# Loading and multiplying the first four x tiles by pairs of feature chunks

## Chip, cores and metric

The kernel runs on one core of one Trainium2 chip. The metric is device time in microseconds, the median of several runs. The engines are TensorE (PE, with its weight loads shown apart as PEld), VectorE (DVE), ScalarE (ACT), GpSimd (POOL) and SyncE (SP), which here only issues DMAs; ACT issues some too.

## What is computed

Two independent parts share one input length of 2048 rows and a width of 1024, and their outputs are joined along the last axis. Part A is a diagonal state-space layer: a complex recurrence over time between two matrix products. Part B is attention over segments of 32 rows with 8 memory rows, whose first step is three projections of the rows:

```python
h = jnp.concatenate([mem, xs], axis=1)
q = jnp.einsum('btd,dhe->bhte', h, Wq)
k = jnp.einsum('btd,dhe->bhte', h, Wk)
v = jnp.einsum('btd,dhe->bhte', h, Wv)
```

The change lies in the start of `v` alone: x is 2048 x 1024, `Wv` is 1024 x 4096 (32 heads of 128).

## The kernel before

**What the start does.** The features (1024) are cut into KC = 8 chunks of 128, the rows into 16 tiles of 128, and the 4096 columns of `Wv` into 8 head blocks (`hb`) of 512. A tile of values is eight matmuls into one PSUM bank, one for each chunk: the stationary operand is a chunk of the turned rows (`b_xe`, features on partitions), the moving one the same chunk of `Wv`'s head block (512 columns). `v_mm` (L414) issues them. Two names of PSUM buffers alternate, psS and psP, with two banks each. Turned rows of tiles 4 to 15 come by DMA transposes (`load_x`, L369); the first four tiles are loaded as they stand (`load_rows`, L372), turned on PE by a product with the identity (`turn_rows`, L379, into psO) and copied to `b_xe` by DVE (L77).

**Loads.** SP and ACT each issue half of the first loads in turn (`q2`): for each tile its rows in two halves of the features, then two chunks of head block 0 of `Wv` (L406). After all four tiles follow head block 1 of `Wv` in two halves of 512 KB, and on SP three loads of 2 KB for `params` (L144), one of 16 KB with the memory rows `mem0` (L906), and five DMA transposes of x. Rows, weights and small loads share one SBUF tile name, `a_hs`. Eight completion semaphores are used in turn, so the third DMA of a queue that reuses one waits for the landing of the earlier DMA.

**Order of the work.** `kernel_main` issues warm-up matmuls on constants (L913), and then draws steps from the generator `values()`: `v_first` (the first four tiles of head block 0), `v_pair` for head block 1 on the same tiles, then both head blocks on the other tiles, then head blocks 2 to 7 between the steps of part A. After the seventh step it calls `params` (its first instruction is the matmul at L150, which turns the three parameter vectors) and `init` (L344, eight small matmuls that turn `mem0`). Matmuls of `v_mm` and transposes of `turn_rows` are held in program order by `keep_in_program_order`; the matmuls of `params` and `init` are not, and a scheduler at build time places them.

In `v_first` each tile is turned when its rows are there, and then those tiles that have been turned are multiplied with the chunks of weights that have been loaded:

```python
for t, todo in enumerate((((0, 0, 2),), ((0, 2, 4), (1, 0, 4)), ((0, 4, 6), (1, 4, 6), (2, 0, 6)),
                          ((0, 6, 8), (1, 6, 8), (2, 6, 8), (3, 0, 8)))):
    self.turn_rows(t, xr)
    for tt, c0, c1 in todo:
        self.v_mm(p[tt], tt, w, range(c0, c1))
```

ACT then copies the four banks to SBUF (L75) and SP stores them to DRAM.

Of the kernel before, what the change touches and what calls it, by code (L numbers as in the profile page):

```python
# [9 lines left out]
BF16 = mybir.dt.bfloat16  # L10
# [306 lines left out]
class PartB:  # L317
# [50 lines left out]
            if lo < hi:  # L368
                k.SP.dma_start(self.xe[:, :, lo:hi], self.x[0][lo + r:hi + r, :], transpose=True)  # L369

    def load_rows(self, t, xr, e, cs=slice(0, D)):
        self.k.tc.keep_in_program_order(e.dma_start(xr[:, t, cs], self.x[0][t * 128 + 64:t * 128 + 192, cs]))  # L372

    def turn_rows(self, t, xr):

        k = self.k
        pt = k.ps("O", (128, 2, 1024), BF16)
        for c in range(KC):
            k.tc.keep_in_program_order(k.PE.transpose(pt[:, c // 4, (c % 4) * 128:(c % 4) * 128 + 128], xr[:, t, c * 128:(c + 1) * 128], k.ident[:]))  # L379
        for i in range(2):  # L380
            k.copy("v", self.xe[:, 4 * i:4 * i + 4, t * 128:(t + 1) * 128], pt[:, i, 0:512].rearrange("p (c n) -> p c n", c=4))

    def sum_x(self, q, pool):

# [59 lines left out]
    def v_first(self, w, xr, e):  # L444

        k = self.k
        p = [k.ps("A") for t in range(4)]
        for t, todo in enumerate((((0, 0, 2),), ((0, 2, 4), (1, 0, 4)), ((0, 4, 6), (1, 4, 6), (2, 0, 6)),
                                  ((0, 6, 8), (1, 6, 8), (2, 6, 8), (3, 0, 8)))):
            self.turn_rows(t, xr)  # L450
            for tt, c0, c1 in todo:
                self.v_mm(p[tt], tt, w, range(c0, c1))
        for q in range(2):
            st = self.v_tile()
            for i in range(2):
                k.copy("s", st[:, i, :], p[2 * q + i][:])
                if i == 0:
                    yield
            self.v_st(0, q, st, e)
            yield  # L460
# [396 lines left out]
def check_consts(k):  # L857

    V, G = k.V, k.G
    k.fmask = k.cst.tile([L, 2, L], FP32, name="f_mask")  # L860
    G.memset(k.fmask[:], 1.0)
    G.affine_select(out=k.fmask[:, 0, :], in_=k.fmask[:, 0, :], compare_op=ALU.is_ge, fill=0.0, base=0,
                    pattern=[[-1, L]], channel_multiplier=1)
    G.memset(k.fmask[0:M, 0, :], 1.0)
    k.tc.keep_in_program_order(V.tensor_scalar(k.fmask[:, 1, :], k.fmask[:, 0, :], 1.0, 1.0e9, ALU.subtract, ALU.mult))


def kernel_main(tc, A_x, A_Lre, A_Lim, A_Bre, A_Bim, A_Cre, A_Cim, A_logdt, A_Dskip, B_x, B_mem0, B_Wq, B_Wk, B_Wv, B_Wo, out,
                force=False, dbg=None):
    with ExitStack() as ctx:  # L870
        k = K(tc, ctx)
# [4 lines left out]
        b = PartB(k, B_x, B_mem0, B_Wq, B_Wk, B_Wv, B_Wo, out)  # L876

        def pool(name, side, bufs=2):
            return tc.tile_pool(name=name, bufs=bufs, side=side, reuse_waits="tile")
# [7 lines left out]
        with pool("p1", "right") as p1:  # L887
            tmp = a.hsp.tile([128, 2 * PC * TB], BF16, name="a_hs", bufs=4)
            w01 = a.hsp.tile([128, 2 * PC * TB], BF16, name="a_hs", bufs=4)
            wvs = {i: w01[:, 4096 * i:4096 * i + 4096].rearrange("p (a b) -> p a b", a=KC) for i in range(2)}  # L890
            st0 = a.hsp.tile([128, 2 * PC * TB], BF16, name="a_hs", bufs=4)
            b.st0 = [st0[:, 1024 * i:1024 * i + 1024].rearrange("p (a b) -> p a b", a=2) for i in range(8)]
            a.pin = b.pin = True
            a.tab = a.wp = a.btp = b.vst = p1
            a.jf = b.rall[:, 0:TB + 1]
            xr = tmp[:, 4096:8192].rearrange("p (t d) -> p t d", t=4)
            q2 = (k.SP, nc.scalar)
            for t in range(4):
                for j in range(2):
                    b.load_rows(t, xr, q2[j], slice(j * 512, j * 512 + 512))  # L900
                for j in range(2):
                    b.load_wv(0, wvs[0], KC, q2[j], [2 * t + j])
            for j in range(2):
                b.load_wv(1, wvs[1], 2, q2[j], [j])
            a.load_params(tmp)
            k.SP.dma_start(tmp[0:M, 0:D], b.mem0[0])  # L906
            b.load_x(512, 1024)
            b.load_x(1024, 1536)
            b.load_x(1536, T)
            one = nc.const_aps.tensor(1.0, [128, 512], BF16)  # L910
            pw = k.ps("O")
            for i in range(7):
                k.PE.matmul(pw[:, i % 2, :], one[:, 0:128], one, start=True, stop=True)  # L913

            def values():
                yield from b.v_first(wvs[0], xr, k.SP)
                for hb, q in [(1, 0), (1, 1)] + [(hb, q) for q in range(2, 8) for hb in range(2)]:
                    yield from b.v_pair(hb, q, wvs[hb], k.SP)
                for hb in range(2, HB):
                    for q in range(8):  # L920
                        if q == 1 and hb + 1 < HB and hb + 1 not in wvs:
                            wvs[hb + 1] = b.load_wv(hb + 1)
                        yield from b.v_pair(hb, q, wvs[hb], k.SP)
            v = values()
            done = 0
            while done < 20:
                next(v); done += 1
                if done == 7:
                    a.params(p1, tmp)
                    b.init(tmp, k.ps('O')[:, 0, :])  # L930
                    a.bt = a.load_b(0)
                    a.load_x(0)
                    tabs = a.tables(0)
                if done == 18:
                    a.load_x(1)
                if done in (9, 14, 17):
                    next(tabs)
                if done in (11, 13, 15, 17, 19):
                    b.sum_x((done - 11) // 2, p1)
            a.tabs = a.ntabs  # L940
            oged = 0
            for n in range(PC * NB):
                pc, tb = n // NB, n % NB
                a.stage1(pc, tb)
                if n in (0, 1):
                    a.load_x(2 + n)
                    wvs[2 + n] = b.load_wv(2 + n)
                if tb == 1 and pc + 1 < PC:
                    nbt = a.load_b(pc + 1)
                want = 20 + 4 * (n + 1) if n < 4 else 36 + (92 * (n - 3) + 27) // 28  # L950
                half = done + 2
                while done < want:
                    next(v, None); done += 1
                    if done == half:
                        a.post(a.prev)
                while done >= 32 and oged < done // 16:
                    b.og(oged, wvs.pop(oged))
                    oged += 1
                if pc + 1 < PC:
                    if tb == 0:  # L960
                        tabs = a.tables(pc + 1)
                    else:
                        next(tabs)
                    if tb == 3:
                        a.tabs, a.bt = a.ntabs, nbt
                if n == 3:
                    a.pin = b.pin = False
                if n == 8:
                    masks(k)
                    check_consts(k)  # L970
                    dB = k.cst.tile([128, D], BF16, name="a_dB")
                    tc.keep_in_program_order(nc.scalar.dma_start(dB[:], A_Dskip.unsqueeze(0).to_broadcast([128, D])))
                if n == 28:
                    a.load_c(0, 0)
                if n == 29:
                    a.load_c(0, 1)
            a.post(a.last)
            k.V.memset(b.rall[:], 0.0)
            a.load_c(1, 0)
            a.load_c(1, 1)  # L980
# [20 lines left out]
        with pool("p3", "right") as p3:  # L1001
# [11 lines left out]
            for n, (hp, u) in enumerate(at):  # L1013
# [4 lines left out]
                if u == 4 and 8 <= hp < 12:  # L1018
                    w = k.w8((8, 512), "wo0")
# [57 lines left out]
@with_exitstack  # L1077
def kernel(
    ctx: ExitStack,
    tc: tile.TileContext,  # L1080
    A_x: bass.AP,
    A_Lambda_re: bass.AP,
    A_Lambda_im: bass.AP,
    A_B_re: bass.AP,
    A_B_im: bass.AP,
    A_C_re: bass.AP,
    A_C_im: bass.AP,
    A_log_dt: bass.AP,
    A_Dskip: bass.AP,
    B_x: bass.AP,  # L1090
    B_mem0: bass.AP,
    B_Wq: bass.AP,
    B_Wk: bass.AP,
    B_Wv: bass.AP,
    B_Wo: bass.AP,
    B_seg_len: bass.AP,
    out: bass.AP,
):
    assert int(B_seg_len) == SEG
    kernel_main(tc, A_x, A_Lambda_re, A_Lambda_im, A_B_re, A_B_im, A_C_re, A_C_im, A_log_dt, A_Dskip,  # L1100
                B_x, B_mem0, B_Wq, B_Wk, B_Wv, B_Wo, out)
# [35 lines left out]
```

## Time and profile before

| what | value |
|---|---|
| median of 5 runs | 1242.49 us (1241.62 to 1242.99) |
| profiled execution, its own time | 1242.26 us |
| its span, first to last instruction | 1240.5 us |
| busy: PE | 1231.4 us (99%) |
| busy: DVE, ACT, POOL | 611.0, 325.9, 199.9 us |
| DMA traffic | 153.95 MB, mean 124 GB/s |
| L414 matmuls, 128x512 | 379 ns in the record, 8 in 1.73 us |
| L379 transposes, 128x128 | 32, the first at 3.8 us, the last at 11.5 us |

Busy time counts an engine's own instructions; a matmul's record is longer than its distance to the next, since they are pipelined. Times in the timelines and in the chain are microseconds from the span's start. A bracket such as [0.50 <-DMA x] says how long the engine had been idle before the instruction, and what ended it.

### The profile page before, as it was taken

How to read it: one execution, taken by the hardware profiler on the slowest of the kernel's cores; microseconds unless marked ns; L12 is line 12 of the kernel's file. 1: busy time of each engine (PE TensorE's matmuls, PEld its weight loads, DVE VectorE, ACT ScalarE, POOL GpSimd, SP SyncE). 2: the span in 40 equal slices, each digit the busy share in tenths (PEclk: the TensorE clock that was granted, in tenths of full speed). 3: DMA queues.
4: the chain of work that ended last, by engine and by line, in shares of the span. 5: the costliest groups of instructions: out<-in, count | busy, mean ns of one | idle time of the engine just before them, and what ended most of it. 6: DMA issues, size and time to landing. Idle time of an engine off the chain costs nothing.

```text
span 1240.5 us, 19641 instructions
## 1 busy us (share of the span) xinstructions
PE 1231.4 (99%) x8078; PEld 655.2 (53%) x8148; DVE 611.0 (49%) x1124; ACT 325.9 (26%) x754; POOL 199.9 (16%) x284
## 2 busy tenths in 40 slices
PE   9999999999999999999999999999999999999998
PEld 4444444444455445566666665655565554454444
DVE  4889999999941122444444444444444550011000
ACT  3344434444310001333333323333333230000000
POOL 2000000000032140222222222222222330000000
PEclk9999999999999999999999999999999999999999
DMA  9942232332656558577768554645575469607000
GB/s 224 262 127 68 85 94 68 102 94 78 152 187 204 157 161 167 103 151 151 141 119 176 120 137 95 129 77 101 106 139 106 72 203 224 147 18 153 17 18 28
DMA packets 306056, 153.95 MB, mean 124 GB/s; under 512 B 147242, under 2 KB 299810, under 8 KB 305962
## 3 DMA queue, kind: packets, MB, share of 16 engines
q1 hardware_dynamic: 304138, 150.82, 52.5%
q10 hardware_dynamic: 1824, 1.84, 0.5%
q8 instruction: 65, 1.06, 0.4%
q14 instruction: 29, 0.24, 0.1%
HBM read 73.70 MB, written 44.71 MB: 95 GB/s over the span
## 4 chain that ended last, share of the span: by engine, by line
PE 99%; DMA 0%; issue 0%; SPq 0%; DVE 0%
PE psP L585 33%; PE psS L685 9%; PE psS L414 9%; PE psP L414 9%; PE psO L256 9%; PE psP L685 5%; PE psP L310 4%; PE psS L310 4%; PE psP L568 4%; PE psO L629 3%; PE psS L611 3%; PE psO L685 2%; PE psS L718 1%; PE psP L505 1%; PE psP L737 1%; PE psO L482 1%
## 5 line engine op out<-in xcount | busy, mean ns | idle before, releaser
L585 PE MATMUL psP<-b_xe,w 128*128 128x480 bf16 x2048 | 439.6, 366 | 0.0
L585 PEld LDWEIGHTS <-w 128*128 128x128 bf16 x2048 | 193.7, 98 | 183.5
L618 POOL TENSOR_TENSOR b_m<-b_e,maskB 99x396 bf16<-99x396 bf16 x160 | 139.4, 871 | 348.2 <-ACT b_e L614 348.2
L77 DVE CAST b_q<-psP 128x480 bf16<-128x480 f32 (+1 forms) x192 | 98.1, 532 | 145.5 <-PE psP L585 134.0
L414 PEld LDWEIGHTS <-b_xe 128*128 128x128 bf16 x1024 | 99.8, 98 | 121.0 <-DVE b_xe L77 1.1
L75 ACT ACTIVATE b_k<-psP 128x480 bf16<-128x480 f32 x128 | 73.1, 571 | 319.1 <-PE psP L585 319.1
L685 PEld LDWEIGHTS <-b_ol 128*128 128x128 bf16 x960 | 93.1, 98 | 109.4
L614 ACT ACTIVATE b_e<-psS 99x396 bf16<-99x396 f32 x176 | 87.4, 497 | 170.9 <-PE psS L611 165.6
L636 DVE TENSOR_TENSOR b_ot<-psO,b_rall 99x512 bf16<-99x512 f32 x176 | 121.7, 691 | 6.4
L256 PE MATMUL psO<-w,a_bt 128*128 128x512 bf16 x496 | 114.7, 379 | 0.8
L634 DVE RECIPROCAL b_rall<-psO 99x4 f32<-99x4 f32 x176 | 31.2, 177 | 132.9 <-PE psO L629 132.9
L685 PE MATMUL psS<-w,b_ol 128*128 128x512 bf16 x406 | 91.5, 379 | 0.6
L414 PE MATMUL psS<-w,b_xe 128*128 128x512 bf16 x378 | 90.1, 379 | 0.4
L414 PE MATMUL psP<-w,b_xe 128*128 128x512 bf16 x376 | 89.8, 379 | 0.4
L256 PEld LDWEIGHTS <-a_bt 128*128 128x128 bf16 x512 | 49.7, 98 | 59.0
L310 PEld LDWEIGHTS <-a_hs 128*128 128x128 bf16 x512 | 49.5, 98 | 58.3
L77 DVE CAST b_ost<-psS 128x512 bf16<-128x512 f32 x13 | 9.0, 692 | 125.4 <-PE psS L685 125.4
L629 PE MATMUL psO<-b_v,b_m 99*128 99x129 bf16 x704 | 70.4, 221 | 0.0
L611 PEld LDWEIGHTS <-b_k 128*128 128x128 bf16 x704 | 50.0, 98 | 33.9 <-DVE b_k L77 0.2
L611 PE MATMUL psS<-b_q,b_k 128*128 128x99 bf16 x704 | 60.1, 208 | 0.1
L75 ACT ACTIVATE b_vst<-psS 128x512 bf16<-128x512 f32 x56 | 33.4, 597 | 99.4 <-PE psS L414 70.2
L310 PE MATMUL psS<-w,a_hs 128*128 128x512 bf16 x245 | 57.3, 379 | 0.6
(203 smaller groups left out, 1095.6 us busy)
## 6 DMA issues: line engine op xcount, KB each, us to landing
b_v<-b_vx SPq DMA_DIRECT2D x16, 1056.0 KB
b_os<-b_ot SPq DMA_DIRECT2D x16, 960.0 KB
w<-in_B_Wv_dram SPq DMA_DIRECT2D x14, 1024.0 KB
b_vx<-b_vst SPq DMA_DIRECT2D x48, 256.0 KB
w<-in_B_Wo_dram SPq DMA_DIRECT2D x12, 1024.0 KB
w<-in_B_Wq_dram SPq DMA_DIRECT2D x16, 512.0 KB
w<-in_B_Wk_dram SPq DMA_DIRECT2D x16, 512.0 KB
a_xn<-in_A_x_dram SPq DMA_DIRECT2D x32, 128.0 KB
```

Of the source, the lines that this page charges most:

```text
L75: self.S.activation(out, in_, ACT.Copy)
L77: self.V.tensor_copy(out, in_)
L256: m = PE.matmul(u[:, i, :], self.bt[:, i, c, :], self.xT[tb][:, c, :], start=(c == 0), stop=(c == KC - 1))
L310: PE.matmul(py[:], self.hs[tb][:, pc, i, tt * 128:(tt + 1) * 128], self.ct[half, i][:, pc, :], start=(pc == 0 and i == 0), stop=(pc == PC ...
L414: m = self.k.PE.matmul(p[:], self.xe[:, c, t * 128:(t + 1) * 128], w[:, c, :], start=(c == 0), stop=(c == KC - 1))
L585: PE.matmul(p[:, 0:480], w[:, i * KC + c, hh * 128:(hh + 1) * 128], self.xe[:, c, 480 * q:480 * q + 480], start=(c == 0), stop=(c == KC - 1))
L611: PE.matmul(s[:, j * GW:(j + 1) * GW], kt[:, hh, g0:g0 + 128], qt[:, hh, g0:g0 + GW], start=True, stop=True)
L614: k.S.activation(e[:], s[0:GW, 0:4 * GW], ACT.Exp, scale=float(E) ** -0.5, accum_out=self.accE[0:GW, i:i + 1])
L618: k.G.tensor_tensor(v4(m[:, 0:4 * GW]), v4(e[:]), mask[0:GW, :, :].unsqueeze(2).to_broadcast([GW, 2, 2, GW]), ALU.mult)
L629: PE.matmul(o[:, gg, cs], m[:, j * GW:j * GW + 128], vt[:, 2 * u + gg, cs], start=True, stop=True)
L636: V.tensor_tensor(ot[:, 2 * u:2 * u + 2, :].rearrange("p g (h e) -> p g h e", h=2), oa[:, :, 1:257].rearrange("p g (h e) -> p g h e", h=2) ...
L685: k.PE.matmul(self.acc[t, half], ol[:, h8, tt * 128:(tt + 1) * 128], self.wo_half(half, h), start=(h == 0), stop=(h == H - 1))
```

## The change

The first four tiles are handled as two pairs of tiles (j = 0, 1) and four pairs of chunks (q = 0 to 3). A row load now brings two tiles with 256 features each, instead of one tile with 512; the bytes of one load stay 128 KB, the contiguous piece falls from 1024 to 512 bytes. The two queues alternate rows and weights: SP has the rows of the first tile pair and the odd chunks of `Wv`, ACT the even chunks and the rows of the second pair. `turn_rows` turns two chunks of two tiles (four transposes) and makes one DVE copy of 512 columns. `v_first` walks over q, with all four tiles at each. There is one warm-up matmul less.

```diff
+    def load_rows(self, j, q, xr, e):
+        cs = slice(256 * q, 256 * q + 256)
+        self.k.tc.keep_in_program_order(e.dma_start(
+            xr[:, 2 * j:2 * j + 2, cs], self.x[0][256 * j + 64:256 * j + 320, cs].rearrange("(i p) d -> p i d", p=128)))
+    def turn_rows(self, j, q, xr):
+        k = self.k
+        pt = k.ps("O", (128, 2, 256), BF16)
+        for c in range(2):
+            for i in range(2):
+                k.tc.keep_in_program_order(k.PE.transpose(
+                    pt[:, c, i * 128:i * 128 + 128], xr[:, 2 * j + i, 256 * q + 128 * c:256 * q + 128 * c + 128], k.ident[:]))
+        k.copy("v", self.xe[:, 2 * q:2 * q + 2, 256 * j:256 * j + 256], pt[:])
...
+        self.turn_rows(0, 0, xr)
+        for q in range(4):
+            if q > 0:
+                self.turn_rows(1, q, xr)
+            for t in range(2):
+                self.v_mm(p[t], t, w, (2 * q,))
+            if q == 0:
+                self.turn_rows(1, q, xr)
+            for t in range(2):
+                self.v_mm(p[t], t, w, (2 * q + 1,))
+            if q < 3:
+                self.turn_rows(0, q + 1, xr)
+            for t in range(2, 4):
+                self.v_mm(p[t], t, w, range(2 * q, 2 * q + 2))
...
-            for t in range(4):
+            for q in range(4):
                 for j in range(2):
-                    b.load_rows(t, xr, q2[j], slice(j * 512, j * 512 + 512))
-                for j in range(2):
-                    b.load_wv(0, wvs[0], KC, q2[j], [2 * t + j])
+                    b.load_rows(j, q, xr, q2[j])
+                    b.load_wv(0, wvs[0], KC, q2[1 - j], [2 * q + j])
...
-            for i in range(7):
+            for i in range(6):
                 k.PE.matmul(pw[:, i % 2, :], one[:, 0:128], one, start=True, stop=True)
```

More of the change, by code (lines that the diff above doesn't have):

```diff
@@ L369, in load_x @@
                 k.SP.dma_start(self.xe[:, :, lo:hi], self.x[0][lo + r:hi + r, :], transpose=True)
-    def load_rows(self, t, xr, e, cs=slice(0, D)):
-        self.k.tc.keep_in_program_order(e.dma_start(xr[:, t, cs], self.x[0][t * 128 + 64:t * 128 + 192, cs]))
-    def turn_rows(self, t, xr):
-        k = self.k
[L377 to L381, printed above, removed]
+    def load_rows(self, j, q, xr, e):
[3 more added lines that the diff above has]
+    def turn_rows(self, j, q, xr):
+        k = self.k
+        pt = k.ps("O", (128, 2, 256), BF16)
[4 more added lines that the diff above has]
+        k.copy("v", self.xe[:, 2 * q:2 * q + 2, 256 * j:256 * j + 256], pt[:])
     def sum_x(self, q, pool):
@@ L447, in v_first @@
         p = [k.ps("A") for t in range(4)]
[L448 to L452, printed above, removed]
+        self.turn_rows(0, 0, xr)
[12 more added lines that the diff above has]
+                self.v_mm(p[t], t, w, range(2 * q, 2 * q + 2))
         for q in range(2):
```

## The prediction

> **What bounds the kernel now.** I read the page's busy shares first, then its chain of waits, then the idle times of PE (TensorE) in order of time.
>
> ```profile
> span 1240.5 us, 19641 instructions
> ...
> PE 1231.4 (99%) x8078; PEld 655.2 (53%) x8148; DVE 611.0 (49%) x1124; ACT 325.9 (26%) x754; POOL 199.9 (16%) x284
> ...
> PE 99%; DMA 0%; issue 0%; SPq 0%; DVE 0%
> ```
>
> PE is the chain: 9.1 us of idle in all. The change can pay only where PE waits, so the question is where those waits lie. The list of waits puts all of PE's longer ones before 15 us; after that its matmuls follow each other to the end. The chain of the first 60 us begins so (start, length, what):
>
> ```profile
> 2.23 4.89 DMA a_hs<-in_B_Wv_dram
> 7.13 0.04 issue
> 7.17 0.59 PE psS L414 x2
> ```
>
> Until 7.17 us PE is short of data; from there it is PE's own work. The PE weight-load timeline shows the two places that matter next (in brackets, idle before, and what ended it):
>
> ```profile
> 14.70 4.86 PEld L414 LDWEIGHTS <-b_xe 128*128 128x128 bf16 x24 [0.50 <-DMA a_hs<-in_B_Wv_dram]
> 19.99 0.09 PEld L150 LDWEIGHTS <-a_hs 24*128 24x128 bf16 x1 [0.42 <-issue]
> 20.00 0.27 PEld L344 LDWEIGHTS <-a_hs 8*128 8x128 bf16 x8
> ```
>
> At 14.70 the next block of Wv (head block 1, chunks 0 to 3) has just landed: the completion record of that DMA on SP's queue ends at 14.66 us. PE had issued its last matmul of the first block at 14.32 and would have been free at 14.54, so 0.17 us was lost there. At 19.99 come the nine small matmuls of `params` (L150) and `init` (L344), 0.31 us from 19.99 to 20.30, with no wait, since their data are long there. What they need is issued on SP behind the weights:
>
> ```profile
> 7.15 0.91 SPq L406 DMA_DIRECT2D a_hs<-in_B_Wv_dram  x2
> 8.10 0.45 SPq L144 DMA_DIRECT2D a_hs<-in_A_Lambda_re_dram  x1
> 8.60 0.28 SPq L144 DMA_DIRECT2D a_hs<-in_A_Lambda_im_dram  x1
> 8.92 0.40 SPq L144 DMA_DIRECT2D a_hs<-in_A_log_dt_dram  x1
> 9.36 0.54 SPq L906 DMA_DIRECT2D a_hs<-in_B_mem_dram  x1
> 10.25 17.11 SPq L369 DMA_TRANSPOSE b_xe<-in_B_x_dram  x5
> ```
>
> The completion record: Wv half 14.66, Lambda_re 14.82, Lambda_im 15.03, log_dt 15.27, mem0 15.55. They come so late because the DMA answer for 7 to 16 us falls from 357 GB/s to 49 just before 14.5 us: 19 packets of the first DMA transpose sit on the engines for up to 1.9 us and end together at 14.52.
>
> **What the Trainium skill says.** "DMA: Bandwidth & Descriptors", Queues, rings and completion order: a DMA's completion increment is an ordered write that lands only after the engine's earlier writes, across its queues. The trace agrees: thirteen engines report the Wv half between 14.52 and 14.66, after the held transposes, and the small DMAs follow at about 0.2 us each. The same page, Specifications, puts full rate at pieces of 512 B and more. The trace has both sizes: in 219 to 222 us, 952 packets of mostly 1024 B with 92.6% of 16 engines, 47 ns each; in 530 to 534 us, 1952 of 512 B with 91.9%, 30 ns each. So 512 B is cheaper per piece and dearer per byte. "TensorE: Matmul & The Clock Gate", Part 1: half clock until about 3.4 us of activity. The trace agrees: start to start 427 ns at first, a last slow one at 5.37 us, 216 ns after (8 in 1.73).
>
> **The change, part by part.**
>
> *One warm-up matmul less* (L913): 0.43 us of PE, ahead of a wait. Before, the seventh ended as the first transpose began (3.79); now the rows set the start (3.57 landed). Gain 0.1 at most, taken up by the waits below.
>
> *Rows in 512 B pieces.* Eight row DMAs of 128 KB keep their bytes, with 16 packets for each engine instead of 8: 64 more packets on each. Price: medians of 27 and 46 ns in the packet record give 2 x 27 - 46 = 8 ns per KB, 64 x 8 = 0.5 us by the end; the loaded averages, 2 x 30 - 47 = 13, give 0.8. Below: nothing, if engines idle between DMAs take it up. I take 0.5. Every later landing on both queues is late by it.
>
> *The order of first work.* 32 transposes, 32 matmuls and 8 copies of 512 columns (0.42 us each) stay; each phase now needs 512 KB for 8 transposes and 8 matmuls. Walk it with the landings of before in the same queue places, plus up to 0.5. Rows (0,0) land 3.6; four transposes at half clock (0.107 each) to 4.15; 0.24 to the copy, copy 0.42, 0.06 to PE: first matmul 4.87 (5.37 before). Two matmuls and the next four transposes to 5.9, two matmuls to 6.3. Rows (0,1), fifth on the queue, land at 6.4 + 0.2, so transposes 6.65 to 6.87. What is left is 28 matmuls x 0.216 = 6.05 and 20 transposes x 0.056 = 1.12, with each later landing ahead of its use (chunk 7: about 11.5, used 12.7) and each copy covered by four or more matmuls: the end is 6.87 + 7.17 = **14.04**, against 14.54. That is a gain of 0.5 on PE alone.
>
> *What is late next.* The half of Wv for head block 1 (14.66 before), and in the built program something that the diff does not show: the scheduler has moved `params` and `init` (L150, L344) on PE from behind three groups of eight matmuls to right behind the first block. They are not pinned, the matmuls around them are. PE runs in order, so the whole of head block 1 is now queued behind mem0's landing, 15.55 before. The added wait replaces the removed one. Nothing on DVE or ACT suffers: `a_raw`, `a_dtb` and `a_rr` move forward with it, and three ACT copies now stand behind `a_rr`, which still comes (1 us after L344) before the first of these groups ends. On SP, B_im's load stands before two stores; its use is at 42.8 us, 10 us later. From 15.5 to the first use of transposed x, seven us of matmuls cover a slip of the transposes.
>
> *When does mem0 land?* Upper: 15.55 + 0.8 = 16.4. The transposes now wait for chunk 7 (10.98 before) instead of chunk 6 (10.23), so they come 0.75 later and can hold completions less. Without any hold, the slowest engine reports the Wv half near 14.4 (the other half's last engine was 14.33) and mem0 0.9 later, 15.3. With 0.5 for the pieces: **15.8**. Lower: the eight engines that carry the 8-row DMAs are not the slowest, and mem0 is there when PE asks, at 14.04.
>
> *Sum.* PE starts head block 1 at mem0 + 0.05 + 0.27. Before, it started at 14.71 and spent 0.31 later on L150 and L344: 15.02 in the same account. Shift = 15.8 + 0.32 - 15.02 = **+1.1 us**. All later PE instructions stand in the same order with no wait, so the shift stays to the end: span 1240.5 + 1.1, the profiled execution's own 1242.26 (1.76 around its span) + 1.1 = 1243.4, and on the median 1242.49, **1243.6 us**.
>
> **Rivals.**
> - *Small loads early.* For it: three engines reported the Wv half already at 12.56 to 12.63. Against: the small DMAs' order behind that half, 0.2 us each. Then L150 and L344 run at 14.04 to 14.35 and the Wv half decides: between 14.4 and 15.2, start 14.45 to 15.25 against 15.02. Shift -0.6 to +0.2, about -0.1: 1242.4.
> - *Slower beyond doubt: pieces paid by number.* In the start-up an engine needs 71 ns per packet (128 packets from 1.9 to 10.98 us), not 46. If that is a price per piece whatever its size, 64 more cost 4.5 us, mem0 lands at 20 and the time is 1247.8. It decides from 25 ns per added packet, where mem0 passes 17.2 and the shift 2.5. Against it: the 30 ns of loaded 512 B packets.
> - *The clock falls back* in PE's new idle of 1.8 us. By the skill's window, half clock for 3.4 us costs 1.7: 1245.3. Against: no gap that long to judge by, but the page of the skill asks for a whole idle window.
> - *The gain as drawn*: waits gone and nothing late, mem0 and the Wv half included. PE is not through before 14.04, so -0.7 at most: 1241.8. Against: those loads stand behind the same 3 MB as before.
>
> **How the numbers follow.** Forecast 0.74, small loads early 0.17, gain as drawn 0.02, pieces by number 0.05, clock 0.02. 0.2% is 2.5 us, about what a measurement of this kernel can tell from no change: forecast, small loads and the gain as drawn lie inside it, the other two above; of the gain as drawn 0.01 is set beyond it, for what I have not seen. Faster 0.01, same 0.92, slower 0.07. The range takes mem0 from 14.2 (-0.5, 1242.0) to 16.4 (+1.7, 1244.2), and scatter (the runs of before spread 1.4): 0.3 below, 0.8 above, where the two upper rivals lie: 1241.7 to 1245.0.
>
> **What would show it.** Right: the first matmul near 4.9; L414's first block over near 14; an idle of 1 to 2 us before L150 or L344 ended by a DMA from log_dt or mem0; head block 1 starting near 16.1, and no new PE wait after it. Wrong: no idle before L344 (first rival); row landings drifting by over 0.2 us per DMA (second); matmuls 427 ns apart after 16 us (clock); or PE waits after 20 us, which I hold to be none.

## The result and the profile after

The median of 24 executions is **1243.65 us** (1243.19 to 1245.45), that of the kernel before, over 44, 1242.37 (1241.49 to 1244.00). The ratio is **1.0011, 95% interval 1.0006 to 1.0017**; drawn again and again from the two lists of times, the difference of the medians is 1.28 us (1.01 to 1.60). So the change costs a little over 1 us. The profiled execution took 1243.63 us.

The head of the page after, and its DMA queues:

```profile
span 1241.8 us, 19638 instructions
...
PE 1232.3 (99%) x8076; PEld 655.8 (53%) x8147; DVE 612.2 (49%) x1124; ACT 326.2 (26%) x754; POOL 199.7 (16%) x284
...
q1 hardware_dynamic: 304650, 150.82, 52.0%
q10 hardware_dynamic: 2336, 1.84, 0.5%
```

The span is 1.3 us longer; PE's busy time grew by 0.9 although two matmul records fewer are in it (a warm-up and a missing record), since a matmul at half clock counts as busy for longer. The two queues of the loads carry 512 packets more each (304138 and 1824 before): 64 for each of the 16 engines.

The weight-load timeline at the place that the prediction named:

```profile
14.04 1.45 PEld L418 LDWEIGHTS <-b_xe 128*128 128x128 bf16 x8
16.02 0.09 PEld L150 LDWEIGHTS <-a_hs 24*128 24x128 bf16 x1 [0.53 <-issue]
16.19 0.26 PEld L344 LDWEIGHTS <-a_hs 8*128 8x128 bf16 x8
16.47 0.98 PEld L418 LDWEIGHTS <-b_xe 128*128 128x128 bf16 x6
```

L150 and L344 (the small matmuls of `params` and `init`) stand at 16.0 to 16.4, ahead of head block 1, which starts at 16.47 instead of 14.71. The completion record (the times at which the DMA engines report a load as done) puts log_dt at 15.91 and mem0 at 16.14. But no wait of one or two microseconds is to be seen: the first block itself was over only at 15.8, 0.3 ahead of mem0. Why, PE's timeline shows:

```profile
4.26 0.61 PE L383 MATMUL psO<-ident,a_hs 128*128 128x128 bf16 x4 [0.70 <-DMA a_hs<-in_B_x_dram]
5.39 0.61 PE L418 MATMUL psS<-a_hs,b_xe 128*128 128x512 bf16 x1 [0.52 <-DVE b_xe L77]
5.79 0.63 PE L418 MATMUL psP<-a_hs,b_xe 128*128 128x512 bf16 x1
6.22 0.63 PE L383 MATMUL psO<-ident,a_hs 128*128 128x128 bf16 x4
6.65 0.63 PE L418 MATMUL psS<-a_hs,b_xe 128*128 128x512 bf16 x1
7.07 0.63 PE L418 MATMUL psP<-a_hs,b_xe 128*128 128x512 bf16 x1
```

Each matmul starts 0.43 us after the last and takes 0.63: half clock, and so it goes on to 9.2. In the kernel before, matmuls stood 0.22 apart from 5.8 on, two of them in 0.59:

```profile
5.37 0.79 PE L414 MATMUL psS<-a_hs,b_xe 128*128 128x512 bf16 x2 [0.52 <-DVE b_xe L77]
7.17 0.59 PE L414 MATMUL psS<-a_hs,b_xe 128*128 128x512 bf16 x2
7.60 0.59 PE L414 MATMUL psP<-a_hs,b_xe 128*128 128x512 bf16 x2
```

The granted clock (PEclk) shows none of this: in both kernels it is 1.00 before 9 us, half-clock matmuls or not, so at a kernel's start the spacing has to be read.

Two things thus came together in this execution: data at 16.1, and a PE that was late by itself. The experiments take them apart.

### The profile page after: what moved, and what is told of

Same layout as the page of the kernel before. It is cut to its first block, busy times and chain, and to the rows that moved or that the text cites. A ratio compares the mean times of both kernels' runs of the same rounds, so it can differ in the third digit from the quotient of the medians.

```text
span 1241.8 us, 19638 instructions
## 1 busy us (share of the span) xinstructions
PE 1232.3 (99%) x8076; PEld 655.8 (53%) x8147; DVE 612.2 (49%) x1124; ACT 326.2 (26%) x754; POOL 199.7 (16%) x284
## 3 DMA queue, kind: packets, MB, share of 16 engines
q8 instruction: 65, 1.06, 0.4%
## 4 chain that ended last, share of the span: by engine, by line
PE 99%; issue 0%; DMA 0%; DVE 0%
PE psP L598 33%; PE psS L698 9%; PE psS L418 9%; PE psP L418 9%; PE psO L256 9%; PE psP L698 5%; PE psP L310 4%; PE psS L310 4%; PE psP L581 4%; PE psO L642 3%; PE psS L624 3%; PE psO L698 2%; PE psS L731 1%; PE psP L518 1%; PE psP L750 1%; PE psO L495 1%
```

## The experiments

Under each, "us" is the median, with the ratio to the kernel before and its 95% interval. Landings come from the completion record.

### The warm-up matmul given back, and two more

```diff
-            for i in range(6):
+            for i in range(7):      # e1_warm7
+            for i in range(9):      # e2_warm9
```

> The changed kernel with its seventh warm-up matmul given back. In the profile of the changed kernel matmuls stayed at 427 ns until about 9.2 us (before: until 5.6), and the first block ended near 15.8. Theory, two waits in a row: the missing warm-up left PE idle from 3.6 to 4.3 us, so that the clock came one window later; given back, the last slow matmul lies before 6.5 us and the first block ends near 14.2, but L150 and L344 still wait for mem0 (16.1 in the changed kernel), head block 1 still starts near 16.4 and the time stays at 1243.6 (within 0.4). Rival, the clock alone made the loss: head block 1 starts near 15 and the time falls to 1242.4. Rival, the warm-up has nothing to do with it: slow to 9 us as in the changed kernel, time as there.

> The changed kernel with nine warm-up matmuls instead of six, so that PE is busy to 4.7 us, past the landing of the first rows (4.2). Same theories as for seven: if idle time ahead of the first transposes decides when the clock is granted, no matmul is 427 ns apart after 6.5 us and the first block ends between 14.2 and 14.6, the time stays near 1243.6 because of mem0. If the clock alone made the loss, 1242.5. If the idle time is not the cause, slow to 9 us, 1243.6 too, but with the first block ending near 15.8.

Measured: seven, 1243.65 us (1.0012, 1.0006 to 1.0019); nine, 1243.17 (1.001, 1.0002 to 1.0018). In the profile with seven the clock still came late (matmuls 427 ns apart to 8.7), the first block's last matmul was issued at 15.24, mem0 landed at 16.09 and head block 1 started at 16.41. With nine the clock was full from 6.2, the block's last matmul was issued at 14.34, and PE then stood until log_dt (15.18) and mem0 (15.41), starting head block 1 at 15.74:

```profile
15.28 0.09 PEld L150 LDWEIGHTS <-a_hs 24*128 24x128 bf16 x1 [1.06 <-DMA a_hs<-in_A_Lambda_re_dram]
15.46 0.26 PEld L344 LDWEIGHTS <-a_hs 8*128 8x128 bf16 x8
15.74 1.84 PEld L418 LDWEIGHTS <-b_xe 128*128 128x128 bf16 x10
```

So in that profile the early clock moved the end of the block and the wait for mem0 took up the gain. By the medians nine warm-ups give back 0.5 us, which the scatter of the executions doesn't tell from nothing.

### The early small matmuls undone, and alone

The move of L150 and L344 ahead of head block 1 is called the hoist here. e3_pin keeps the changed kernel and holds them at their old place in PE's order; e4_before_hoist takes the kernel before and puts them where the change did.

```diff
-        PE.matmul(pr[:, 0:3 * PC], r24, ...)
+        k.tc.keep_in_program_order(PE.matmul(pr[:, 0:3 * PC], r24, ...))      # both, and so at L344
...
-                if done == 7:
+                if done == 4:                                                  # e4 alone
                     a.params(p1, tmp)
                     b.init(tmp, k.ps('O')[:, 0, :])
+                if done == 7:
```

> The changed kernel with the matmuls of params and init held behind three groups of head block 1, where they stand in the kernel before. Theory, two waits: mem0's wait is gone, head block 1 starts when the first block is over and its half of Wv has landed (15.1): with a slow clock to 9 us at 15.85, a shift of +1.1 against the kernel before, 1243.5; with a clock granted at 5.6 at 15.15, +0.4, 1242.8. Rival, mem0's place on PE alone made the loss: back to 1242.4 whatever the clock.

> The kernel before with one edit: params and init are called, and held, right behind the first block, as the scheduler placed them in the changed kernel. Theory: PE waits at L344 for mem0, 15.55 in the profile of before; head block 1 starts at 15.9 instead of 14.71 and L150 and L344 no longer cost 0.31 later: +0.85, 1243.2 us. Rival, the position is free (their loads are there by then, the loss of the change is the clock): hb 1 starts at 14.9 or earlier, 1242.4.

Measured: e3 1242.96 us (1.0005, 0.9997 to 1.0014), e4 1243.19 (1.0006, 0.9998 to 1.0014). By their medians the hoist alone costs 0.8 us, and taking it out of the changed kernel gives back 0.7 of 1.28. Both intervals just take in a ratio of 1; drawn again from the two lists of times, as above, the 0.8 has 0.41 to 1.17 and the 0.7 has 0.2 to 0.9. The weight loads of e3 and of e4:

```profile
15.32 2.06 PEld L418 LDWEIGHTS <-b_xe 128*128 128x128 bf16 x11 [0.87 <-DMA a_hs<-in_B_Wv_dram]
```

```profile
14.48 0.09 PEld L150 LDWEIGHTS <-a_hs 24*128 24x128 bf16 x1 [0.54 <-DMA a_hs<-in_A_Lambda_re_dram]
14.69 0.26 PEld L344 LDWEIGHTS <-a_hs 8*128 8x128 bf16 x8
14.97 2.49 PEld L414 LDWEIGHTS <-b_xe 128*128 128x128 bf16 x13
```

In e3 head block 1 waits for its own weights and starts at 15.32, while mem0 landed at 16.10: with the hoist it would have started 1.1 us later, less the 0.4 that the nine small matmuls take further on instead. Its clock came early, yet its first block was over only at 14.79, because PE waited 1.1 us, to 12.82, for the last load of rows. In e4's profile the landings were early (mem0 14.64), and that execution, 1242.04 us, is the quickest of its thirteen; the median lies 1.15 above.

### The changed kernel once more

> The changed kernel once more, for the profile alone. If the moment when the clock is granted belongs to the run and not to the kernel, the last slow matmul lies elsewhere than at 8.8 us, while head block 1 still starts at mem0's landing plus 0.3, between 15.3 and 16.6. If it belongs to the kernel (six warm-ups, the idle time before the first rows), it is at 8.8 again.

One execution, 1243.92 us. PE's waits and the chain show what the first profile hid:

```profile
PE psO L150 <- DMA a_hs<-in_A_log_dt_dram: 1.1, 1, 1.1
```

```profile
9.08 7.17 DMA a_hs<-in_A_log_dt_dram
16.25 0.14 issue
16.39 0.18 PE psO L150
```

The block's last matmul was issued at 14.91, log_dt landed at 16.25, mem0 at 16.53, and head block 1 started at 16.86. This is the predicted wait: PE done and idle for 1.1 us, a small load ending it, the whole of head block 1 queued behind.

### Rows in pieces of 512 bytes, old order

```diff
-        self.k.tc.keep_in_program_order(e.dma_start(xr[:, t, cs], self.x[0][t * 128 + 64:t * 128 + 192, cs]))
+        g = cs.start // 256
+        self.k.tc.keep_in_program_order(e.dma_start(xr[:, t, g:g + 2, 0:256],
+            self.x[0][t * 128 + 64:t * 128 + 192, cs].rearrange("p (g d) -> p g d", g=2)))
...
```

The tile of rows is padded so that the two pieces of a row do not lie side by side; the transposes read it accordingly.

> The kernel before with one edit: each row load writes its 512 features as two pieces of 256 into a padded tile, so that it moves 512-byte pieces; order of loads, transposes and matmuls as before. Theory: 64 more packets for each engine at 8 ns make the half of Wv for head block 1 land 0.5 later (about 15.2, before 14.66) and mem0 near 16.0; L150 stands three groups later and does not wait; head block 1 starts 0.5 later, 1242.9. Rival, pieces of 512 bytes cost nothing in the start-up: landings and time as before, 1242.4. Rival, paid by number: Wv half at 18 and 1245 or more.

Measured: 1242.66 us, 1.0001 (0.9993 to 1.001). The pieces are not paid by number (that was 4.5 us), but 0.5 and nothing both lie inside the interval. The profile shows no delay: the last half of head block 1 landed at 14.10 and mem0 at 14.99, earlier than in the kernel before (14.66 and 15.55). The loads by themselves were repeated, in outline:

```python
for n in range(16):        # even n: 1024 B row pieces in the old order; odd n: 512 B in the new
    rows, head block 0, two halves of head block 1, four small loads   # no transposes, no matmuls
```

> Computes nothing of the reference and writes zeros: it repeats the start's 3 MB of loads 16 times on the same two queues (rows, head block 0 of Wv, the halves of head block 1, then the four small loads on SP), each repeat held until the one before has landed. Even repeats use the old row loads (1024 B pieces) in the old order, odd ones the new row loads (512 B pieces) in the new order. No DMA transposes are in it. Mine: the last landing of rows and chunks is 0 to 0.5 us later in the odd repeats (64 more packets for each engine x 8 ns = 0.5). Rival, pieces cost nothing: no difference over the scatter. Rival, pieces paid by number: odd repeats 4.5 us later. On the hold by the transposes: without them mem0 should land before the slower half of Wv's head block 1 or within 0.5 us behind it in most repeats, since the eight engines of the small loads are not tied to the slowest one; if it comes about 0.9 us behind as in the kernels (14.66 to 15.55), the transposes are not what makes it late.

Over eight repeats of each kind, the last of the 16 row and chunk loads landed 11.76 us after the first issue with 1024 B and 12.23 with 512: 0.47 later, with a standard error of 0.53. The slower half of head block 1 came 0.49 later (0.25), mem0 0.45 (0.40), the rows that the first transposes need 0.49 (0.27). Four readings near 0.5, none of them sharp, and not independent: 4.5 is out, and nothing is not excluded. The repeats change the order of the loads together with the pieces, so they price the two together; e5, with the new pieces in the old order, leaves open which of the two it is.

### The DMA transposes moved behind the start

Both kernels with L150 and L344 held in their old place, and the loads of x by DMA transpose (and part A's behind them, which are held in order too) issued only after the first store of values.

```diff
-            b.load_x(512, 1024); b.load_x(1024, 1536); b.load_x(1536, T)
...
+                if done == 2:
+                    b.load_x(512, 1024); b.load_x(1024, 1536); b.load_x(1536, T)
```

> As e3_pin, and the DMA transposes of x (and part A's behind them) are issued on SP only after the first store of values, so that nothing holds the completions of the Wv half. Theory: the transposes held these completions (ten of sixteen engines reported together at 14.96 to 15.08 in the changed kernel); without them the Wv half lands at 14.5 or earlier, head block 1 starts when the first block ends, 14.1 to 14.6 with an early clock, 15.8 with a late one: 1242.3, about 0.6 below e3_pin. Rival, bytes alone set the landing: 15.1 as before, time as e3_pin. Rival, the late transposes are missed at the third pair of tiles (21.5 us): PE waits there, above 1243.5.

> The kernel before with the same late DMA transposes, params and init held where they stood. Theory: the Wv half lands before 14.3 and the wait of 0.17 at 14.7 is gone: -0.1 to -0.3, 1242.2, which these runs can hardly tell from no change; the view to read is the landing. Rival, bytes alone: landing at 14.7, 1242.4. Rival, transposes too late: PE waits near 21.5, above 1243.

Measured: e8 (changed kernel) 1244.3 us (1242.47 to 1247.37), 1.0015 (1.0007 to 1.0023); e9 (kernel before) 1242.40, 0.9999 (0.999 to 1.0007). The weight loads at the start of head block 1, e8 and then e9:

```profile
14.98 2.49 PEld L418 LDWEIGHTS <-b_xe 128*128 128x128 bf16 x13 [1.88 <-DMA a_hs<-in_B_Wv_dram]
```

```profile
15.70 1.84 PEld L414 LDWEIGHTS <-b_xe 128*128 128x128 bf16 x10 [1.41 <-DMA a_hs<-in_B_Wv_dram]
```

In e9 mem0 landed at 14.70, one microsecond *ahead* of the last half of `Wv` (15.66), where in the kernel before it came 0.9 behind (15.55 after 14.66); in e8 it came 0.4 behind (15.34 after 14.94). In the repeated loads, also without transposes, mem0 lies from 1.04 ahead to 0.74 behind the slower half, 0.13 behind on average. In the eight profiles with the transposes in their place it is 0.55 to 1.06 behind. So without the transposes the small loads lag less behind `Wv` on average. That they then land earlier by the clock is not shown: 15.34 in e8 is close to 15.41, the earliest of the new order with them, and e4 had 14.64 in the old order with them. `Wv` itself is no earlier without them: its last half landed at 14.94 and 15.66. Why e8 is slower and so spread is open; its profile shows no wait of PE after 20 us, but it is that of one of the two quickest executions (1242.47).

### When does the full clock come?

Two kernels repeat only PE's activity of the start. In m2_clock the old and the new order follow each other, in m3_idle the warm-ups and the idle behind them vary (the lists are m3's):

```python
PAT = ((8, 0), (7, 16), (6, 16), (6, 512), (6, 1024))   # warm-ups, width of the DVE copy that makes PE wait
MID = (16, 512, 1024, 2048)                             # the same for the wait ahead of the last 24 matmuls
```

> Computes nothing of the reference and writes zeros: 32 repeats of PE's activity of the start without any DMA, after an idle of some 13 us or more whose length grows, in four patterns in turn: b7 (seven warm-ups, eight transposes, copy, two matmuls, eight transposes, copy, 24 matmuls), a6, a7 and a9 (six, seven or nine warm-ups, then four transposes, copy, two matmuls, four transposes, two matmuls, four transposes, 24 matmuls). Read: the time from the first warm-up to the first two matmuls 216 ns apart. Mine[...]: in each pattern it scatters over about 3.4 us from repeat to repeat (some 3.5 to 7), and the means of the four patterns differ by less than 1 us. Rival, the shorter warm-up and the gaps of the new order make the clock late: a6 is later than b7 in nearly all repeats by 2 us or more, and a9 is back at b7's. Rival, a fixed delay from first activity: each pattern's values agree within 0.5 us.

> Computes nothing of the reference and writes zeros: 60 repeats of PE's start without DMA loads, each after an idle of 8 us or more. Five starts in turn: eight warm-ups with no idle before the first transposes; seven and an idle of about 0.5 us; six and 0.5; six and 1.0 (what the changed kernel has); six and 1.5. Then four transposes, copy, two matmuls, 2 x (four transposes, two matmuls), 40 matmuls, an idle of 0.5, 1.0, 1.5 or 2 us in turn (the changed kernel waits 1 to 2 us there), 24 matmuls. Theory, from the repeats without DMA before (six warm-ups and 1.0 us of idle: full clock only 7 us or more after the first warm-up in 7 of 8; seven and 0.5: 2 of 8; no idle: 0 of 16): the idle ahead of the transposes makes the grant late, in at most 1 of 12 repeats without idle, 2 to 5 of 12 at 0.5 and 9 or more of 12 at 1.0 and 1.5. Rival, the number of warm-ups decides: six with 0.5 is late as often as six with 1.0. Rival, chance of the run alone: all five alike. On the second idle: if the clock falls back in a wait of 1 to 2 us, which would explain the few executions 1.7 us above the rest, the 24 matmuls behind it show 427 ns in some of the 15 repeats of each length, more at 2 us; if not, none does.

The time from the first warm-up to matmuls 216 ns apart was 3.9 to 6.6 us or 7.1 to 9.9 (the 60 repeats of m4 below, 3.9 to 6.8). How often it was over 7, with the distance from the last warm-up's start to the first transpose (0.43 means that PE goes straight on):

| start | over 7 us |
|---|---|
| nine or eight warm-ups, 0.43 us (no idle; m2, m3, m4) | 0 of 8, 0 of 12, 0 of 60 |
| old pattern, seven and eight transposes, 0.43 (no idle; m2) | 0 of 8 |
| seven, 0.90 us (m2, m3) | 2 of 8, 5 of 12 |
| six, 0.90 us (m3) | 12 of 12 |
| six, 1.41 us (m2, m3) | 7 of 8, 11 of 12 |
| six, 1.96 us (m3) | 10 of 12 |

PE's timeline in two repeats of m3, six and seven warm-ups with the same idle (pw are the warm-ups, pt the transposes, pm the other matmuls):

```profile
73.04 2.72 PE L59 MATMUL pw<-one,xe 128*128 128x512 bf16 x6 [7.93 <-DVE one L72]
76.03 0.61 PE L63 MATMUL pt<-ident,rows 128*128 128x128 bf16 x4 [0.27 <-DVE rows L78]
...
79.69 3.62 PE L59 MATMUL pm<-one,xe 128*128 128x512 bf16 x10
```

```profile
198.17 3.14 PE L59 MATMUL pw<-one,xe 128*128 128x512 bf16 x7 [7.98 <-DVE one L72]
201.58 0.47 PE L63 MATMUL pt<-ident,rows 128*128 128x128 bf16 x4 [0.27 <-DVE rows L78]
...
203.90 2.32 PE L59 MATMUL pm<-one,xe 128*128 128x512 bf16 x10
```

The first ten of the 40 matmuls behind the transposes take 3.62 us against 2.32, and the last of the 40 starts 16.4 us after the first warm-up instead of 14.1. What I had come to believe from the kernels' profiles, that the moment is chance of the run alone, falls. So does the theory written down for m3, that the idle alone decides: at the same idle of 0.90, six warm-ups are late in 12 of 12 and seven in 7 of 20. But seven with no idle are late in none of 8. The table orders itself by *how long PE had worked without a break before the first idle*, with the transposes that follow directly counted in: 3.8 us or more (eight warm-ups and four transposes, seven and eight, nine and four) never late, 3.0 sometimes, 2.6 nearly always. Six without an idle and eight with one were not run. The kernels are milder than m3: of four profiles with six warm-ups (distances 1.03 to 1.33) two were late and two early, and in e1_warm7 seven (0.87) were late.

### When does it fall back?

> Computes nothing of the reference and writes zeros: 60 repeats like those of the idle study, all with eight warm-ups and no idle before the transposes, and before the last 24 matmuls a spacing of about 1.7, 1.9, 2.1, 2.3 and 2.5 us in turn (from the last matmul before to the first after). Before, a spacing of 1.62 left the clock full in 15 of 15 and one of 2.54 brought it down in 9 of 15, each time with 1.68 us more for the 24 matmuls. Theory, the wait that the change added on mem0 (0.98 and 1.48 us in the traces, up to about 2 when the clock comes early and mem0 late) can cost this too: the share that falls rises steadily from 0 at 1.62, so that 1 to 4 of 12 fall at 1.9 and 3 to 6 at 2.1. Rival, a threshold near 2.4: none falls up to 2.3, and the few executions 1.7 us above the rest have another cause.

m3 and m4 have 24 matmuls behind a second wait. The spacing is from the start of the last matmul before it to the start of the first behind it. Up to a spacing of 2.08 us the 24 took 4.97 us from first to last start in every repeat (45 in m3, 36 in m4); at 2.37, 3 of 12, and at 2.54, 9 of 15 (m3) and 2 of 12 (m4) took 6.65. The theory of a steady rise from 1.62 falls. Which of these 39 repeats fell back is not chance either: it goes with the time from the moment of full clock to the last matmul before the wait. All 13 with 7.1 to 7.6 or 9.7 us fell, and of the 26 with 7.8 to 9.1 one did. PE's timeline in m4 at 2.08, then at 2.37 (one record of 24 is missing in each):

```profile
91.29 5.35 PE L59 MATMUL pm<-one,xe 128*128 128x512 bf16 x23 [1.70 <-DVE xe L88]
```

```profile
120.73 7.04 PE L59 MATMUL pm<-one,xe 128*128 128x512 bf16 x23 [2.00 <-DVE xe L88]
```

The price is 1.68 us, as in the prediction's rival. A kernel had it once, in the profile of e5_before_512 (1243.88 us, the slowest of its executions), after PE's thin work from 5.3 to 7.2 us, where no spacing was over 1.37. Two stretches of it (from:to and length in us, PE's busy time and instructions, granted clock, DMA share, GB/s):

```profile
6.20:7.20 1.00, 0.53 (x8) 1.00 1.12 351
7.20:10.60 3.40, 3.32 (x16) 0.55 0.89 270
```

A few executions with the hoisted wait lie some 1.7 us above the rest (1245.1 to 1245.8: 3 of 24 of the changed kernel, 3 of 21 with seven warm-ups, 2 of 13 with nine; none of the 13 each of e3 and e4). The amount is that of a fall-back, and the mean granted clock points the same way: in the six of the changed kernel and of seven warm-ups it is 0.998, in every other execution of these two kernels 0.999 or 1.0 (with nine the two have 0.999, as three others have). None of them was profiled, and the longest spacing of the hoisted wait in a profile is 1.48 us, where no fall was seen. So a fall-back in the new wait is likely for them, and not shown.

## Why the prediction was right

**The wait.** Right, and by the medians the main cost. It put the hoist at 15.55 + 0.32 - 15.02 = 0.85 us in landings of before; alone it measured 0.8. The 0.31 in 15.02 is read a little short: in the kernel before, the matmul ahead of L150 starts at 19.68, so the next was due at 19.90 and came at 20.30. The nine small matmuls cost 0.40 there, which makes the hoist 0.76. "mem0 + 0.32" held in each of four profiles: 16.14 to 16.47, 16.53 to 16.86, 16.09 to 16.41, 15.41 to 15.74.

**mem0's landing.** Taken as 15.8, measured 15.41 to 16.53 in these four, on average 16.04; one of four lies above the upper end of 16.4.

**The pieces.** Taken as 0.5; 0.45 to 0.49 in the repeated loads, with errors from half as large to as large, and there together with the order of the loads. Hoist and pieces together, 0.7 to 0.8 and 0.5, come to the 1.28 measured. That the 0.6 left in e3 is the pieces, and no part of it the clock, was not shown.

**The first block over at 14.04.** Wrong: 15.8 and 15.1 in the two profiles of the changed kernel, 15.5 with seven warm-ups, 14.55 with nine. Two terms failed. The walk took full clock from about 6 us on, near where it was before. It had read the trace of before as agreeing with about 3.4 us of half clock, though the slow matmul at 5.37 lies 4.5 us after the first: the moment was not to be counted on. And "one warm-up matmul less, gain 0.1 at most" looked at 0.43 us of PE and not at what those matmuls are for. Taken away ahead of an idle, it can hold the clock back (full from 9.2 and 8.1 us in those two profiles, 6.2 with nine), and with it the end of the block. The second is the first rows: they landed at 3.95 to 4.22, not 3.6, so the first matmul came at 5.39 and 5.12 instead of 4.87. The walk itself was not too quick: in e8, with an early clock, the first matmul came at 4.88 and the block was over at 13.44. In e3 a third term failed, the landing "ahead of its use" (the 1.1 us for rows). In all four profiles of the changed order with the hoisted wait the block was still over before mem0 landed, so this error was covered by the wait that the forecast had right. That is luck: in the first profile 0.3 us more would have let PE, not mem0, set the start. With the wait gone the error would count.

**What makes the small loads late.** Half right at most: without the transposes mem0 lags less behind `Wv` (1.0 ahead in one profile, 0.4 behind in the other), but `Wv`'s half is as late without them, so that these completions are held by the transposes is not borne out.

**The rivals.** Small loads early: not in any profile of the changed kernel's loads with the transposes in their place. Pieces by number: out. The gain as drawn: out, and even with an early clock (nine warm-ups, PE through at 14.5) it was spent in the wait for mem0. The clock: in the profiles it came late at the start rather than falling back in the new wait; in 3 of the 24 executions it may have fallen back there. What the late start costs in the median was not measured by itself. No PE wait after 20 us: right; from there the chain is matmul after matmul.

No run has nine warm-ups and the small matmuls held in place in one kernel, the kernel before with six warm-ups, the new order with 1024 B rows, or head block 1 in smaller loads. So the clock's share and the pieces' share of what e3 keeps are not told apart.

## What to carry to other kernels

When a change reorders work, look at the built order for instructions that are not pinned: here nine small matmuls moved ahead of a block and tied it to the last of the small loads, by the medians some 0.8 of the 1.28 us. A warm-up matmul is not priced by its own time: with eight and no idle behind them the full clock came within 6.8 us in all 72 repeats, with six ahead of an idle it came after 7 us in 40 of 44. And an earlier finish is worth only the distance to the next thing that is late.

## What the runs showed of the hardware

- The full clock came early (within 6.8 us of the first matmul) in 72 of 72 repeats that began with 3.8 us of PE work without a break (eight warm-ups, then four transposes), and in 4 of 44 after 2.6 us (six) and an idle. With seven and an idle both kinds occur, 4.2 to 4.5 and 7.9 to 9.9 us.
- Back to half clock, in m3 and m4: never up to a spacing of 2.08 us between matmuls (81 repeats), in 14 of 39 at 2.37 and 2.54, for 1.68 us each time. I had expected nothing below 3.4 us. With thin work before it, a kernel fell back with no spacing over 1.37.
- The granted clock in the kernels' profiles reads 1.00 through the first half-clock phase, and 0.55 when it falls back later. In m3 it reads 0.50 in the half-clock phase of a later repeat (73.0 to 75.9 us).
- The slower half of head block 1 landed between 13.75 and 15.66 us in the ten profiles, all with the same bytes issued ahead of it: a wider spread than any effect of the change.
